# Sixteen softplus stores issued from ScalarE's queue instead of the sync engine's

## The chip, the cores and the metric

The kernel runs on one core of a Trainium2 chip. The metric is the device time of one execution in microseconds (us), as the median of several runs. Engines are named as in the profile: PE is TensorE (matmuls), PEld its weight loads, DVE is VectorE, ACT is ScalarE, POOL is GpSimd and SP is the sync engine, which here only issues DMAs. A name with a q behind it (SPq, ACTq) is the engine's sequencer, which waits for semaphores and issues DMAs.

## The reference

Three layers follow each other, on 2304 tokens of 512 features:

```python
x = attn(q, k, v, omega)            # random-feature attention, 4 x 8 heads x 576 x 64 -> (2304, 512)
h = x @ w_in                        # (2304, 512) @ (512, 2048)
g = maximum(h, 0) + log1p(exp(-abs(h)))   # softplus
x = g @ w_out                       # (2304, 2048) @ (2048, 512)
out = ((x @ w1) * (x @ w2) @ w3) @ w_out2   # 512 -> 1024 -> 1024 -> 512
```

## The kernel before, in words

Everything is kept transposed: features on the 128 partitions, tokens along the free axis. Each fp32 operand of a matmul is split into a high and a low part (`hi`, `lo`), ACT casting the high part and DVE subtracting it for the low one, and each product is three matmuls (`mm3`, line L87 in the profile).

**The softplus layer** (`widen(Up1, ...)`). The 2048 output features are 8 column pairs `i` (two blocks of 128 each), the tokens 3 chunks `c` of 768 (two halves of `N` = 384). One pair and one chunk make a quad (i,c): a two by two block product that is done with seven products and additions. `begin` does four of the seven products, copies one of them out of PSUM (`p6`, L482, on ACT), adds on DVE (`u2`, `u3`, `c22`, L475) and puts the first result; `finish` does the other three and puts three more. `put` is a softplus on ACT (L507) and a store of 128 x 384 to the DRAM tile `gd` (L508). `widen` begins a quad before it finishes the one ahead of it. The order of the last six quads is (6,0), (6,1), (7,0), (7,1), (6,2), (7,2).

**The down projection** (`down`, first use `d1`) reads `gd` back in tiles `dn` of 128 x 512 (L574, issued by SP), splits each into `dhi` (ACT, L581) and `dlo` (DVE, L582), and multiplies with `w_out`. Its `seq` takes the first two token groups together, so the `dn` tiles alternate between tokens 0 to 511 and 512 to 1023, and each tile has 12 matmuls. It loads four tiles ahead (`AHEAD`), and these four loads and the first two splits are written just before the last two quads are finished (`before_last`); the fifth load on stands in the loop behind the quads.

**Weights** are prepared on the way. A `Job` loads a raw 64-bit tile (L120, issued by ACT) and turns it into fp32 with one ACT operation (L127) and four DVE operations (L130, L136, L143, L150), then splits it (ACT L176, DVE L181). In the stretch around the change these are the jobs of `w_out`; `step(rate)` hands out such operations between products.

**What sets the order.** The framework draws up each engine's instruction list when the kernel is built, from data dependences, free buffers and priorities; `tc.high_priority(URGENT)` puts the softplus, the additions and the splits of `dn` 300 places ahead of where they are written, while stores and loads keep their own place. On the chip each engine, and each DMA queue, takes its list in order. The tiles `c22`, `c21`, `c12`, `c11`, `p6`, `u2`, `u3`, `dn`, `dhi` and `dlo` all come from one pool of 14 buffers (`M_`), and a buffer comes free when its last reader is done, for a softplus result when its store has landed.

Of the kernel before, what the change touches and what calls it, by code (L numbers as in the profile page):

```python
# [31 lines left out]
KD, NF, NJ = DM // 128, FF1 // 128, FF2 // 128  # L32
# [12 lines left out]
N = 384  # L45
# [17 lines left out]
def body(ctx: ExitStack, tc: tile.TileContext, q, k, k_rest, v, v_rest, om_t, w_in, w_out, w12, w3, wo, out):  # L63
    nc = tc.nc
# [32 lines left out]
    gd = [dr.tile([128, NT], F32, name=f"gd{f}") for f in range(NF)]  # L97
# [14 lines left out]
    class Job:  # L112
        def __init__(self, src, n, place, pool, sums=False):
            self.src, self.n, self.place, self.pool, self.sums, self.done = src, n, place, pool, sums, False
            self.slots = 4 if sums else 2
            self.kept = self.queue = None
# [382 lines left out]
    class Up1(Quad):  # L499
        def __init__(self, i, c, rate):  # L500
            super().__init__(win[i], xo[c], rate)
            self.i, self.t = i, 2 * N * c

        def put(self, dst, src, f, t):
            t = self.t + t * N
            with tc.high_priority(URGENT):
                nc.scalar.activation(out=dst, in_=src, func=AF.Softplus)  # L507
            nc.sync.dma_start(out=gd[2 * self.i + f][:, t:t + N], in_=dst)  # L508

        def begin(self):  # L510
            super().begin()
# [371 lines left out]
```

## Time and profile before

| what | value |
|---|---|
| median of 3 runs | 866.73 us (866.51 to 868.63) |
| the profiled execution's own time | 865.56 us |
| its span, from the first to the last instruction | 863.7 us |
| PE busy | 845.2 us, 98% of the span |
| DVE busy | 605.7 us, 70% |
| ACT busy | 381.8 us, 44% |
| mean granted PE clock | 0.996 of full speed |
| `gd` stores (L508), all issued by SP | 96, 192 KB each, median 2.6 us to landing |

The page gives busy time by engine over the whole span. Matmuls are pipelined, so a busy PE isn't PE at its peak, and idle time of an engine that isn't the bottleneck costs nothing. The softplus quads run from about 159 us (the first L507) to 338 us (the last L508), the first down projection from there to about 574 us.

### The profile page before, as it was taken

How to read it: one execution, taken by the hardware profiler on the slowest of the kernel's cores; microseconds unless marked ns; L12 is line 12 of the kernel's file. 1: busy time of each engine (PE TensorE's matmuls, PEld its weight loads, DVE VectorE, ACT ScalarE, POOL GpSimd, SP SyncE). 2: the span in 40 equal slices, each digit the busy share in tenths (PEclk: the TensorE clock that was granted, in tenths of full speed). 3: DMA queues.
4: the chain of work that ended last, by engine and by line, in shares of the span. 5: the costliest groups of instructions: out<-in, count | busy, mean ns of one | idle time of the engine just before them, and what ended most of it. 6: DMA issues, size and time to landing. Idle time of an engine off the chain costs nothing.

```text
span 863.7 us, 14514 instructions
## 1 busy us (share of the span) xinstructions
PE 845.2 (98%) x5496; PEld 760.6 (88%) x5496; DVE 605.7 (70%) x1007; ACT 381.8 (44%) x796; POOL 43.5 (5%) x35
## 2 busy tenths in 40 slices
PE   8999999989999998999999999999999999999998
PEld 7888888989999996888888888899999999988887
DVE  5678798978888789887876767279996655653322
ACT  6686889554444555444433432254311111232221
POOL 3512230000000000000000000000000000000000
PEclk9999999999999999999999999999999999999999
DMA  8622344564454568657687764154232211454433
GB/s 305 237 92 76 117 153 138 159 238 159 165 190 157 177 216 283 204 187 248 200 268 246 246 223 152 41 192 165 104 104 80 80 56 55 160 176 147 146 123 98
DMA packets 72534, 141.67 MB, mean 164 GB/s; under 512 B 7056, under 2 KB 39952, under 8 KB 69392
## 3 DMA queue, kind: packets, MB, share of 16 engines
q1 hardware_dynamic: 65984, 102.99, 35.7%
q10 hardware_dynamic: 6480, 37.75, 13.1%
q8 instruction: 43, 0.70, 0.3%
q14 instruction: 27, 0.22, 0.1%
HBM read 94.05 MB, written 46.66 MB: 163 GB/s over the span
## 4 chain that ended last, share of the span: by engine, by line
PE 81%; DVE 4%; DMA 3%; issue 1%; ACT 1%; SPq 0%; DVEq 0%; ACTq 0%
PE ps L87 80%; DMA xq<-xd 2%; PE ps L368 1%; PE ps L398 1%; DMA raw<-in_w_in 1%; DVE s L423 1%; DVE c L475 0%; DMA dn<-gd 0%; DMA gd<-c 0%; DVE f L143 0%; DVE u L475 0%; DVE nmax L309 0%; DVE xt L389 0%; DVE lo L181 0%; DVE dlo L582 0%
## 5 line engine op out<-in xcount | busy, mean ns | idle before, releaser
L87 PE MATMUL ps<-dlo,hi 128*128 128x512 f32 (+1 forms) x320 | 120.2, 376 | 2.9 <-DVE dlo L582 2.9
L87 PE MATMUL ps<-dhi,hi 128*128 128x512 f32 (+1 forms) x320 | 119.5, 376 | 1.6 <-ACT dhi L581 0.9
L87 PE MATMUL ps<-dhi,lo 128*128 128x512 f32 (+1 forms) x320 | 119.9, 375 | 0.0
L582 DVE TENSOR_TENSOR dlo<-dn,dhi 128x512 fp32r<-128x512 f32 (+1 forms) x120 | 74.8, 636 | 60.2 <-ACT dhi L581 33.5
L581 ACT CAST dhi<-dn 128x512 fp32r<-128x512 f32 (+1 forms) x120 | 67.4, 577 | 72.8 <-DVE dlo L582 35.4
L87 PEld LDWEIGHTS ps<-dlo,hi 128*128 128x128 f32 x320 | 60.6, 189 | 15.5 <-DVE dlo L582 3.9
L87 PEld LDWEIGHTS ps<-dhi,hi 128*128 128x128 f32 x320 | 60.3, 189 | 15.0 <-DVE c L475 1.6
L475 DVE TENSOR_TENSOR c<-ps,u 128x384 f32<-128x384 f32 x144 | 71.6, 549 | 0.6
L87 PEld LDWEIGHTS ps<-dhi,lo 128*128 128x128 f32 x320 | 60.6, 189 | 11.7
L482 ACT COPY p<-ps 128x384 f32<-128x384 f32 x48 | 22.8, 475 | 99.5 <-PE ps L87 78.0
L475 DVE TENSOR_TENSOR u<-ps,p 128x384 f32<-128x384 f32 x48 | 26.7, 555 | 56.5 <-PE ps L87 55.6
L507 ACT ACTIVATE c<-c 128x384 f32<-128x384 f32 x72 | 35.3, 522 | 67.4 <-DVE c L475 56.0
L130 DVE SCALAR_TENSOR_TENSOR f<-raw,f 128x1024 f32<-128x1024 f32 (+2 forms) x43 | 45.7, 1066 | 27.0 <-ACT f L127 26.9
L127 ACT ACTIVATE f<-raw 128x1024 f32<-128x1024 f32 (+2 forms) x43 | 42.4, 992 | 44.1 <-DMA raw<-in_w 36.2
L309 DVE TENSOR_REDUCE nmax<-ps 128x4 f32<-128x512 f32 x72 | 48.1, 682 | 18.5 <-PE ps L87 11.9
L87 PE MATMUL ps<-dhi,w34l 128*128 128x512 f32 (+1 forms) x160 | 59.6, 373 | 0.0
L87 PE MATMUL ps<-dlo,w34h 128*128 128x512 f32 (+1 forms) x160 | 59.6, 372 | 0.0
L87 PE MATMUL ps<-dhi,w34h 128*128 128x512 f32 (+1 forms) x160 | 59.1, 373 | 0.0
L176 ACT CAST hi<-f 128x1024 fp32r<-128x1024 f32 (+2 forms) x42 | 38.4, 918 | 40.1 <-DVE f L150 20.5
L181 DVE TENSOR_TENSOR lo<-f,hi 128x512 fp32r<-128x512 f32 (+3 forms) x58 | 42.0, 745 | 6.9 <-ACT hi L176 6.9
L143 DVE SCALAR_TENSOR_TENSOR f<-raw,f 128x1024 int32<-128x1024 int32 (+2 forms) x43 | 45.3, 1056 | 0.6
L150 DVE SCALAR_TENSOR_TENSOR f<-raw,f 128x1024 int32<-128x1024 int32 (+2 forms) x43 | 44.9, 1046 | 0.4
(147 smaller groups left out, 2112.2 us busy)
## 6 DMA issues: line engine op xcount, KB each, us to landing
gd<-c SPq DMA_DIRECT2D x96, 192.0 KB, 2.6
dn<-gd SPq DMA_DIRECT2D x64, 256.0 KB, 3.5
raw<-in_w ACTq DMA_DIRECT2D x16, 1024.0 KB, 6.0
pd<-c SPq DMA_DIRECT2D x48, 192.0 KB, 1.9
dn<-pd SPq DMA_DIRECT2D x32, 256.0 KB, 3.3
raw<-in_w_out ACTq DMA_DIRECT2D x10, 768.0 KB, 4.5
raw<-in_w_in ACTq DMA_DIRECT2D x6, 1024.0 KB, 5.6
rawq<-in_q SPq DMA_DIRECT2D x18, 256.0 KB, 3.7
```

Source lines behind the costliest of these rows:

```text
L87: nc.tensor.matmul(out=o, lhsT=a, rhs=b, start=start, stop=stop, **kw)
L127: nc.scalar.activation(out=self.f, in_=self.words(1, F32), func=AF.Relu, scale=-1.0)
L130: nc.vector.scalar_tensor_tensor(out=self.f, in0=self.words(1, F32), scalar=SMALLEST, in1=self.f, op0=ALU.max, op1=ALU.max)
L143: nc.vector.scalar_tensor_tensor(out=fi, in0=self.words(1, I32), scalar=-0x40000000, in1=fi, op0=ALU.bitwise_and, op1=ALU.bitwise_or,)
L150: nc.vector.scalar_tensor_tensor(out=fi, in0=self.words(0, I32), scalar=29, in1=fi, op0=ALU.logical_shift_right, op1=ALU.bitwise_or,)
L176: nc.scalar.copy(out=self.hi, in_=self.f)
L181: nc.vector.tensor_tensor(out=self.lo[:, a:b], in0=self.f[:, a:b], in1=self.hi[:, a:b].bitcast(F32), op=ALU.subtract)
L309: nc.vector.tensor_reduce(out=nmax, in_=pj, axis=AX.X, op=ALU.max, negate=True)
L475: nc.vector.tensor_tensor(out=z, in0=bank, in1=y, op=ALU.add)
L507: nc.scalar.activation(out=dst, in_=src, func=AF.Softplus)
L581: nc.scalar.copy(out=hi, in_=got[m])
L582: nc.vector.tensor_tensor(out=lo, in0=got.pop(m), in1=hi.bitcast(F32), op=ALU.subtract)
```

## The change

The stores of the quads with `i` of 6 or 7 and `c` of 1 or 2 are issued by ACT (`nc.scalar`) and not by SP (`nc.sync`). That is four quads of four stores each. Their sources, destinations and sizes stay as they are, and the other 80 stores stay on SP.

```diff
         def __init__(self, i, c, rate):
             super().__init__(win[i], xo[c], rate)
             self.i, self.t = i, 2 * N * c
+            self.queue = nc.scalar if i >= NF // 2 - 2 and c else nc.sync
 
         def put(self, dst, src, f, t):
             t = self.t + t * N
             with tc.high_priority(URGENT):
                 nc.scalar.activation(out=dst, in_=src, func=AF.Softplus)
-            nc.sync.dma_start(out=gd[2 * self.i + f][:, t:t + N], in_=dst)
+            self.queue.dma_start(out=gd[2 * self.i + f][:, t:t + N], in_=dst)
```

## Rows read from the trace of the kernel before

**Rows 1.** Windows: stretch, length, busy PE, PEld, DVE, ACT, POOL, clock, DMA share, GB/s.
```profile
178.00:316.00 138.00, 137.66 (x792) 137.48 (x793) 114.37 (x183) 68.06 (x126) 0.00 (x0) 1.00 0.53 182
...
316.00:318.00 2.00, 2.00 (x13) 2.00 (x12) 1.61 (x3) 0.16 (x1) 0.00 (x0) 1.00 0.00 0
...
329.50:342.00 12.50, 8.31 (x31) 4.81 (x29) 12.05 (x18) 8.21 (x15) 0.00 (x0) 1.00 0.78 253
342.00:346.60 4.60, 4.60 (x14) 3.60 (x14) 3.43 (x5) 2.70 (x5) 0.00 (x0) 0.63 1.04 378
346.60:574.00 227.40, 227.37 (x1029) 185.40 (x1027) 157.75 (x211) 89.38 (x135) 0.00 (x0) 1.00 0.62 204
```

**Rows 2.** Timeline of PE, 329 to 344 us: start, duration, instruction, idle before.
```profile
330.37 0.73 PE L87 MATMUL ps<-dhi,hi 128*128 128x512 f32 x2 [0.57 <-ACT dhi L581]
...
341.92 0.50 PE L87 MATMUL ps<-dlo,hi 128*128 128x512 f32 x1 [2.22 <-DVE dlo L582]
...
343.67 0.63 PE L87 MATMUL ps<-dlo,hi 128*128 128x512 f32 x1
```

**Rows 3.** Timeline of DVE in the same stretch.
```profile
329.84 0.96 DVE L130 SCALAR_TENSOR_TENSOR f<-raw,f 128x768 f32<-128x768 f32 x1 [0.50 <-ACT f L127]
...
338.45 0.95 DVE L181 TENSOR_TENSOR lo<-f,hi 128x768 fp32r<-128x768 f32 x1
```

**Rows 4.** Groups by line on DVE, 329.5 to 342 us: count, busy us, mean ns.
```profile
L130 DVE SCALAR_TENSOR_TENSOR f<-raw,f 128x768 f32<-128x768 f32 x2 | 1.9, 956 | 0.5 <-ACT f L127 0.5
...
L136 DVE TENSOR_SCALAR f<-f 128x768 int32<-128x768 int32 x2 | 1.1, 555 | 0.0
```

**Rows 5.** Timeline of ACT and its sequencer, 322 to 339 us.
```profile
322.96 0.33 ACTq L120 DMA_DIRECT2D raw<-in_w_out  x1
326.98 0.53 ACT L507 ACTIVATE c<-c 128x384 f32<-128x384 f32 x1 [3.25 <-DVE c L475]
328.91 0.91 ACT L127 ACTIVATE f<-raw 128x768 f32<-128x768 f32 x1 [1.40 <-DMA raw<-in_w_out]
...
334.80 0.91 ACT L127 ACTIVATE f<-raw 128x768 f32<-128x768 f32 x1
335.82 1.00 ACT L507 ACTIVATE c<-c 128x384 f32<-128x384 f32 x2
...
337.10 0.84 ACT L176 CAST hi<-f 128x768 fp32r<-128x768 f32 x1
337.11 0.33 ACTq L120 DMA_DIRECT2D raw<-in_w_out  x1
337.84 1.14 ACT L581 CAST dhi<-dn 128x512 fp32r<-128x512 f32 x2
```

**Rows 6.** Landing, us: raw loads of 322.96 and 317.90, first two `dn` loads.
```profile
raw<-in_w_out ACTq DMA_DIRECT2D x1, 768.0 KB, 5.9
...
raw<-in_w_out ACTq DMA_DIRECT2D x1, 768.0 KB, 4.1
...
DMA to landing us min/median/max: 3.4/3.8/4.2
```

**Rows 7.** Timeline of SP's queue, 322 to 345 us (merged runs of one line).
```profile
322.06 1.03 SPq L574 DMA_DIRECT2D dn<-gd  x2
327.54 0.32 SPq L508 DMA_DIRECT2D gd<-c  x1
327.95 0.87 SPq L574 DMA_DIRECT2D dn<-gd  x2
333.93 4.67 SPq L508 DMA_DIRECT2D gd<-c  x6
338.69 6.38 SPq L574 DMA_DIRECT2D dn<-gd  x6
```

**Rows 8.** Line L508, 296 to 340 us: ns min/median/max of one issue.
```profile
L508 SPq DMA_DIRECT2D gd<-c x23: 319/383/1275, 298.3 to 338.2; - x23
```

**Rows 9.** Line L166, all of its issues: ns min/median/max.
```profile
L166 ACTq DMA_DIRECT2D wf<-f x4: 366/432/468, 448.9 to 508.4; - x4
```

## The prediction

> **What bounds the kernel now.** I read the busy time by stage first. TensorE (PE) is the bound nearly everywhere: from 178 to 316 us, through the quads of the softplus layer, it is busy for 137.66 of 138.00 us, and from 346.6 to 574 us, in the first down projection, for 227.37 of 227.40 [rows 1]. Between them lies one knot, from 329.5 to 342 us, where the last quads end and the down projection starts: PE is busy there for 8.31 of 12.50 us, and VectorE (DVE) for 12.05. All sixteen moved stores are issued before the end of this knot, so what the change can do to the time, it does by moving the point at which PE restarts for good, 341.92 us [rows 2].
>
> Next the timeline of PE: the longest of its waits, 2.22 us, ends at 341.92 with the low part `dlo` of the third `dn` tile, and a matmul of 343.67 us takes 0.63 us where that of 341.92 took 0.50; the mean granted clock of 342 to 346.6 us is 0.63 [rows 1], so part of this stretch, right behind an idle PE, ran at the lower of the two levels (1.2 GHz). So the most that a perfect knot could give back is 12.50 - 8.31 = 4.19 us of idle time and 4.60 x (1 - 0.63) = 1.70 us of clock: 5.9 us, 0.68% of the span. Within 0.3%, or 2.6 us, is what I count as no change.
>
> Then what `dlo` waits for. The idle time of DVE in the knot, 12.50 - 12.05 = 0.45 us, is one piece, the end of the 0.50 us before 329.84, where its L130 waits for ScalarE's (ACT's) L127 [rows 3]; from there on it is gapless. Its list there is not only urgent work: two of each of L130, L136, L143 and L150 prepare `w_out` for later (L143 and L150 take 0.95 us, as L130 does) [rows 4]. Before that L127 ACT sat idle 1.40 us for the raw weight tile, whose load was issued at 322.96 us [rows 5] and took 5.9 us, where the load before it took 4.1 [rows 6].
>
> Last the queue of the sync engine (SP). It issues in order, and a store waits there for its softplus, so what is queued behind it waits too: the loads of the third and fourth `dn` tile go at 327.95, behind a store of 327.54, and the loads from the fifth on at 338.69, behind six stores that begin at 333.93 [rows 7].
>
> **The change part by part.** It moves sixteen stores, those of the quads (6,1), (7,1), (6,2) and (7,2), at a median of 0.383 us of issue each [rows 8], from SP to ACT: 6.1 us. Nothing is computed differently, and no bytes are added.
>
> *Off SP.* Left in front of the first `dn` loads are the stores of (7,0) alone. The DMA engines moved 0 GB/s from 316 to 318 us [rows 1], so the first four `dn` loads (1 MB in all) can start there, as far as their buffers are free, and not two from 322.06 and two from 327.95 [rows 7]. Their own landing was not what PE waited for: the first two landed 4.2 us after their issue at the latest [rows 6], by some 326.8, and PE started on the first at 330.37 [rows 2], when ACT had cast it; and PE needs the fifth only after the 24 matmuls of the third and fourth. So the earlier loads by themselves give 0. Indirectly they clear the way for the raw tile: two of them no longer run beside it, and I let it take the 4.1 us of its neighbour. It lands at 327.1 and not at 328.9; L127 then starts behind the softplus that ends at 327.51 [rows 5], ends at 328.4, and L130 follows the instruction before it without the 0.50 us of idle time. From there DVE is gapless to the `dlo` on which PE restarts: -0.50 us. The 0.57 us that PE waited for the first cast [rows 2] also goes, but PE only comes sooner to the same wait; it is not added. The dip of the clock I leave as it is. The bounds of this term are 0 (the loads wait for buffers, and the raw tile is as late as before) and -0.50.
>
> *Onto ACT, in the PE-bound stretch.* Nine of the sixteen fall before 322 us. If a store is put right behind its softplus, ACT's sequencer waits out the 0.53 us of it [rows 5] and issues for 0.38, where the next softplus would have started after 0.47 (two in a row take 1.00): 0.44 us, with the hand-over 0.5 each, and 2 us in a quad of 42 matmuls, 42 x 138.00 / 792 = 7.3 us. ACT is busy for 68.06 of 138.00 us there [rows 1], 3.6 in a quad, so 5.6 of 7.3 are full; PE, which never idles there, covers it. Without that cover the nine would cost 4.5 us. The raw load of 322.96 stands on the same queue and could slip by some 0.6 us; the margin that the 4.1 us leave (1.8 us) takes it.
>
> *Onto ACT, in the knot.* Seven are left: one behind the softplus of 326.98, where ACT idles 1.40 us anyway, and twice three. Cheapest: each is issued beside a running ACT operation, as the raw load at 337.11 goes beside the cast of 337.10, with the next cast at 337.84, before that one has ended (337.10 + 0.84) [rows 5]; the stores that ACT issues already, L166, take 0.37 to 0.47 us of issue [rows 9], also less than a cast. Then the cost is 0. With each three in a clump behind its last softplus it is more: with everything 0.50 us earlier, the first clump ends at about 335.1, L127 (0.91) goes from 335.1 to 336.0, the softplus from 335.82 on, three by 337.10, go from 336.0 to 337.3, the second clump ends at 338.15, and the cast L176 of 337.10, which would have gone at 336.6, ends at 339.0. DVE's L181, due at 338.45 - 0.50 = 337.95 [rows 3], starts 1.1 us late, and `dlo` with it. Dearest: seven times 0.5 us and one long issue (1.275 us at the worst [rows 8], 0.9 above the median), all in series: 4.4 us. I take 0: the rows in which ACT issues a DMA are nearest, and all show it beside a running operation. The clump's +1.1 stays in the forecast's own range.
>
> Sum: -0.50 + 0 = -0.5 us. The profiled execution took 865.56 us (span 863.7), the median of the runs is 866.73; both lie on the same kernel, and the difference is put on the median: 866.2. The forecast's own range, with both bounds of both terms, is 866.2 to 867.8 (0 and +1.1).
>
> The page "DMA: Bandwidth & Descriptors" of the Trainium skill, section "Issuing engines are not separate DMA queues", speaks against a gain: DMAs from SP and from ScalarE run on the same 16 engines, and starting them from several places saves only the sequencer's issue time. By that rule the change would save SP 6.1 us that no wait of PE shows, and the time would stay at 866.7. The row of the SP queue shows something beside it, that a load was held not by issue time but by a waiting store.
>
> **The rivals.**
>
> *The knot comes loose (faster).* Each engine's order is drawn up when the kernel is built, by priority and readiness, and the preparation of `w_out` fills holes in it. The sixteen issues now fill holes on ACT that L127 (334.80) and L176 (337.10) filled. If this L127 falls behind the casts of the third `dn` tile, the four DVE operations that hang on it (3 x 0.956 + 0.555 = 3.4 us [rows 4]) fall behind `dlo` too. They stand in front of it now, and its cast was done at about 338.5. Then the 2.22 us wait closes, the dip of the clock behind it (1.70) need not come, and with the 0.50 the time is 866.7 - 4.4 = 862.3. For it speaks that DVE alone holds `dlo`; against it that the third cast, at 337.84, needs PE to have finished with earlier tiles, which no queue changes.
>
> *ACT becomes the knot (slower).* A store that stands right behind its softplus stops every later cast on ACT, and the casts feed DVE, which has no slack in the knot. It decides from 2.6 + 0.5 = 3.1 us on, which is six of the seven stores exposed at 0.5 us and a little of a long issue; in full it is 4.4 - 0.5 = +3.9: 869.3 to 870.6. For it: the softplus that a store waits for ends later than the next one could start. Against it: ACT is busy for only 8.21 of 12.50 us in the knot [rows 1], so some of the stores fall into idle time.
>
> *Nothing moves.* The loads wait for buffers, the stores for ACT's holes, and the static order of DVE stays: 866.7.
>
> **How the numbers follow.** The forecast (866.2 and its clump variant) gets 0.38, nothing moves 0.18, the knot comes loose 0.28, ACT becomes the knot 0.16. Hence faster by over 0.3% 0.28, within 0.56, slower 0.16. The likeliest is 866.2. The range reaches from 862.0, just past the loose knot at its worked-out size (what it leaves out there is a knot that closes wholly, down to 866.7 - 5.9 = 860.8, some 0.06), to 869.5, where ACT as the knot begins; most of that case, 0.14, stays out.
>
> **What would show it.** The loads L574 of the first `dn` tiles issued before 320 us, from an SP without waits between them; the raw load of about 322.9 landing in some 4 us; no idle time of DVE at its L130; PE's last wait of the knot still about 2 us and ending 0.5 us earlier; sixteen ACT issues of L508, each about 0.38 us. Wrong would be: the order of L130 to L150 against `dlo` L582 changed, the clock's dip gone or a second one there, the waits of ACT's L176 or L581 on its own stores in place of DVE, or PE idle before 329 us, which would put the nine earlier stores on the path.

## The result, and the profile after

The change made the kernel faster: 860.37 us (857.63 to 862.58, 6 runs) against 867.68 us (864.68 to 872.78, 6 runs) for the kernel before on the same chip. The ratio is 0.9916, with a 95% interval of 0.9888 to 0.9944, so 7.3 us less, of which the interval allows 4.9 to 9.7. The forecast was 866.2, that is 0.5 us less than the 866.73 it was worked out from, with a range from 862.0 to 869.5: the time lies below the range. The profiled execution took 857.63 us, with a span of 855.6.

In `after` the lines behind 502 are numbered one higher: L507 is L508, L508 is L509, L574, L581 and L582 are L575, L582 and L583. The kernels of the experiments have some lines more, so their numbers are shifted a little further; the names of the tiles tell which line is meant.

Windows of the changed kernel (columns as in [rows 1]). The knot begins about 1 us earlier here, which comes from the attention stage and not from the change, so its window does too:

```profile
178.00:316.00 138.00, 138.00 (x796) 137.82 (x795) 112.18 (x181) 67.41 (x125) 0.00 (x0) 1.00 0.52 183
...
328.50:341.00 12.50, 11.61 (x50) 9.13 (x50) 11.50 (x18) 7.12 (x14) 0.00 (x0) 1.00 0.83 286
...
346.60:574.00 227.40, 227.40 (x1061) 187.02 (x1060) 167.05 (x224) 92.50 (x142) 0.00 (x0) 1.00 0.62 209
```

PE is busy in the knot for 11.61 of 12.50 us, where it was 8.31, and the lower clock behind it is gone. DVE is busy between 346.6 and 574 us for 9.3 us more than before (167.05 against 157.75 [rows 1]). That stretch of time doesn't hold the same work in both kernels, since the changed one is some 7 us ahead there. So here is DVE (third of the busy times) between the same two matmuls of the down projection, the 97th and the 941st, in the kernel before (first line) and in the changed one:

```profile
359.43:581.81 222.38, 222.10 (x1037) 182.63 (x1036) 152.55 (x204) 86.68 (x132) 0.00 (x0) 1.00 0.61 202
352.23:574.06 221.83, 221.83 (x1038) 182.57 (x1037) 163.29 (x219) 90.18 (x138) 0.00 (x0) 1.00 0.62 209
```

It is 10.7 us more, while PE takes no longer: work has moved from in front of the 97th matmul to behind it.

The timeline of PE from the last matmuls of the quads on:

```profile
328.51 0.33 PE L87 MATMUL ps<-xa12h,lo 128*128 128x384 f32 x1
328.68 0.63 PE L87 MATMUL ps<-dhi,hi 128*128 128x512 f32 x2
...
332.53 0.50 PE L87 MATMUL ps<-dhi,hi 128*128 128x512 f32 x1 [0.89 <-ACT c L508]
...
336.36 0.40 PE L87 MATMUL ps<-dlo,hi 128*128 128x512 f32 x1
```

PE goes from the quads into the down projection without a wait. The kernel before had five, here by what ended them (sum, number, longest):

```profile
PE ps L87 <- DVE dlo L582: 2.6, 2, 2.2
PE ps L87 <- ACT dhi L581: 0.9, 2, 0.6
PE ps L87 <- DVE c L475: 0.7, 1, 0.7
```

One is left, 0.89 us in the place of the 0.7, and the third tile's `dlo` makes none.

The timelines of DVE and of ACT show why:

```profile
327.03 1.29 DVE L583 TENSOR_TENSOR dlo<-dn,dhi 128x512 fp32r<-128x512 f32 x2 [0.24 <-ACT dhi L582]
328.24 1.02 DVE L475 TENSOR_TENSOR c<-ps,u 128x384 f32<-128x384 f32 x2
329.17 0.95 DVE L130 SCALAR_TENSOR_TENSOR f<-raw,f 128x768 f32<-128x768 f32 x1
...
334.22 0.69 DVE L583 TENSOR_TENSOR dlo<-dn,dhi 128x512 fp32r<-128x512 f32 x1 [0.97 <-ACT dhi L582]
```

```profile
326.39 0.60 ACT L582 CAST dhi<-dn 128x512 fp32r<-128x512 f32 x1
...
326.90 0.62 ACT L582 CAST dhi<-dn 128x512 fp32r<-128x512 f32 x1
327.42 0.90 ACT L127 ACTIVATE f<-raw 128x768 f32<-128x768 f32 x1
330.37 0.91 ACT L127 ACTIVATE f<-raw 128x768 f32<-128x768 f32 x1 [2.05 <-DMA raw<-in_w_out]
331.19 0.92 ACT L508 ACTIVATE c<-c 128x384 f32<-128x384 f32 x2
...
333.58 0.61 ACT L582 CAST dhi<-dn 128x512 fp32r<-128x512 f32 x1
```

The first cast, the first `dlo` and the third `dlo` (with the fourth) in the kernel before, from its timelines of ACT and of DVE:

```profile
329.71 0.61 ACT L581 CAST dhi<-dn 128x512 fp32r<-128x512 f32 x1
```

```profile
330.72 0.68 DVE L582 TENSOR_TENSOR dlo<-dn,dhi 128x512 fp32r<-128x512 f32 x1
...
341.18 1.29 DVE L582 TENSOR_TENSOR dlo<-dn,dhi 128x512 fp32r<-128x512 f32 x2
```

The first two tiles are split while PE still works on the quads. Before, an L127 that waited for its raw tile stood in front of the first cast, and an L130 in front of the first `dlo` [rows 3, 5]. Not the speed of an operation has changed but the place at which it stands. How far the preparation of the weights had come is counted by L150, the last operation of each job: those that start ahead of the first `dlo`, in the kernel before (first fence) and in the changed one:

```profile
L150 DVE SCALAR_TENSOR_TENSOR f<-raw,f x13: 948/959/1224, 186.5 to 328.4; 128x768 int32<-128x768 int32 x7, 128x1024 int32<-128x1024 int32 x6
```

```profile
L150 DVE SCALAR_TENSOR_TENSOR f<-raw,f x12: 946/1086/1225, 185.6 to 323.2; 128x1024 int32<-128x1024 int32 x6, 128x768 int32<-128x768 int32 x6
```

The count begins at 178 us. Thirteen became twelve: at the first `dlo` the preparation is one `w_out` job behind, which is five DVE operations of some 4.4 us in all (with the split L181).

The two queues, in the changed kernel's timeline of SP and its lines of L509:

```profile
297.75 14.48 SPq L509 DMA_DIRECT2D gd<-c  x7
313.94 35.77 SPq L575 DMA_DIRECT2D dn<-gd  x14
```

```profile
L509 SPq DMA_DIRECT2D gd<-c x80: 319/384/2164, 160.8 to 311.8; - x80
...
L509 ACTq DMA_DIRECT2D gd<-c x16: 326/359/871, 297.8 to 335.8; - x16
```

SP's last store is the one of 311.8 us, and its loads go from 313.94 on, before 320 us as forecast; an issue takes ACT's sequencer 0.36 us at the median.

**A measure for the knot.** Whole runs of one kernel spread by several us, so the profiles are compared by one stretch: from the start of the last matmul of the quads to the start of the 97th of the down projection. Without any wait it takes 0.17 + 96 x 0.233 = 22.5 us, from the steps between the starts of matmuls.

| kernel | from, us | to, us | stretch | PE idle in it | L150 ahead of the first `dlo` | ratio of times to the kernel before on the same chip, 95% interval |
|---|---|---|---|---|---|---|
| before | 329.46 | 359.43 | 29.97 | 4.18 | 13 | |
| before again (e12) | 330.69 | 360.63 | 29.94 | 4.34 | 13 | 1.0023 (0.9993 to 1.0053) |
| change | 328.51 | 352.23 | 23.72 | 0.89 | 12 | 0.9916 (0.9888 to 0.9944) |
| change again (e5) | 334.42 | 358.04 | 23.62 | 0.78 | 12 | 0.9930 (0.9899 to 0.9961) |
| e1 loads on GpSimd | 330.74 | 359.64 | 28.90 | 4.70 | 13 | 1.0030 (0.9995 to 1.0064) |
| e2 one job held | 333.30 | 359.70 | 26.40 | 2.29 | 13 | 0.9980 (0.9950 to 1.0011) |
| e3 two jobs held | 331.53 | 356.86 | 25.33 | 1.99 | 13 | 0.9955 (0.9923 to 0.9986) |
| e4 stores on GpSimd | 332.04 | 357.65 | 25.61 | 1.64 | 13 | 0.9992 (0.9966 to 1.0017) |
| e6 order only | 333.60 | 356.32 | 22.72 | 0 | 12 | 0.9924 (0.9899 to 0.9949) |
| e7 change, old order | 332.57 | 357.02 | 24.45 | 1.34 | 12 | 0.9934 (0.9907 to 0.9960) |
| e8 change, L127 held | 332.12 | 354.69 | 22.57 | 0 | 12 | 0.9907 (0.9871 to 0.9944) |
| e9 second chunk only | 332.54 | 358.06 | 25.52 | 1.63 | 12 | 0.9946 (0.9921 to 0.9970) |
| e10 third chunk only | 329.53 | 354.00 | 24.47 | 1.65 | 12 | 0.9945 (0.9917 to 0.9973) |
| e11 all stores on ACT | 331.62 | 354.39 | 22.77 | 0 | 10 | 0.9925 (0.9898 to 0.9953) |

The ratios are worked out over the runs and need not be those of the two medians. Of the 7.3 us, 29.97 - 23.72 = 6.25 us lie in this stretch; the rest is inside the interval. Each row rests on one profile, but both kernels that were profiled twice give the same stretch to 0.1 us.

### The profile page after: what moved, and what is told of

It is laid out like the page before. It is cut to its first block, busy times and chain, and to the rows that moved or that the text cites. A ratio compares the mean times of both kernels' runs of the same rounds, so it can differ in the third digit from the quotient of the medians.

```text
span 855.6 us, 14492 instructions
## 1 busy us (share of the span) xinstructions
PE 841.4 (98%) x5496; PEld 759.4 (89%) x5496; DVE 605.4 (71%) x1007; ACT 380.8 (45%) x796; POOL 44.0 (5%) x35
## 4 chain that ended last, share of the span: by engine, by line
PE 85%; DMA 2%; DVE 2%; issue 1%; ACT 1%; ACTq 0%; DVEq 0%
PE ps L87 83%; PE ps L368 1%; DMA xq<-xd 1%; PE ps L398 1%; DMA raw<-in_w_in 1%; DMA raw<-in_w_out 1%; DVE s L423 0%; DVE u L475 0%; DVE xa22l L433 0%; DVE nmax L309 0%; DVE t L157 0%; DVE xt L389 0%; DVE f L143 0%; ACT c L508 0%; ACT qp L314 0%
## 5 line engine op out<-in xcount | busy, mean ns | idle before, releaser
L583 DVE TENSOR_TENSOR dlo<-dn,dhi 128x512 fp32r<-128x512 f32 (+1 forms) x120 | 74.9, 635 | 65.4 <-ACT dhi L582 39.9
L582 ACT CAST dhi<-dn 128x512 fp32r<-128x512 f32 (+1 forms) x120 | 67.2, 576 | 59.9 <-DVE dlo L583 32.6
L87 PEld LDWEIGHTS ps<-dhi,lo 128*128 128x128 f32 x320 | 60.2, 188 | 11.7
L482 ACT COPY p<-ps 128x384 f32<-128x384 f32 x48 | 22.8, 475 | 99.1 <-PE ps L87 77.9
L508 ACT ACTIVATE c<-c 128x384 f32<-128x384 f32 x72 | 35.2, 521 | 65.9 <-DVE c L475 54.6
L130 DVE SCALAR_TENSOR_TENSOR f<-raw,f 128x1024 f32<-128x1024 f32 (+2 forms) x43 | 45.7, 1066 | 17.2 <-ACT f L127 17.0
L127 ACT ACTIVATE f<-raw 128x1024 f32<-128x1024 f32 (+2 forms) x43 | 42.3, 991 | 29.9 <-DMA raw<-in_w 21.3
L181 DVE TENSOR_TENSOR lo<-f,hi 128x512 fp32r<-128x512 f32 (+3 forms) x58 | 42.0, 745 | 8.0 <-ACT hi L176 8.0
L150 DVE SCALAR_TENSOR_TENSOR f<-raw,f 128x1024 int32<-128x1024 int32 (+2 forms) x43 | 45.0, 1046 | 0.5
```

Of the source, the lines that this page charges most:

```text
L87: nc.tensor.matmul(out=o, lhsT=a, rhs=b, start=start, stop=stop, **kw)
L127: nc.scalar.activation(out=self.f, in_=self.words(1, F32), func=AF.Relu, scale=-1.0)
L130: nc.vector.scalar_tensor_tensor(out=self.f, in0=self.words(1, F32), scalar=SMALLEST, in1=self.f, op0=ALU.max, op1=ALU.max)
L150: nc.vector.scalar_tensor_tensor(out=fi, in0=self.words(0, I32), scalar=29, in1=fi, op0=ALU.logical_shift_right, op1=ALU.bitwise_or,)
L181: nc.vector.tensor_tensor(out=self.lo[:, a:b], in0=self.f[:, a:b], in1=self.hi[:, a:b].bitcast(F32), op=ALU.subtract)
L582: nc.scalar.copy(out=hi, in_=got[m])
```

## The experiments

The theories are named in the expectations. **A**: the gain lies in the order in which the instruction lists of DVE, ACT and PE are drawn up, and the moved stores act by changing that order. **B**: it lies on the chip, in loads and buffers that no longer stand behind waiting stores in SP's queue. **B2** is B as a helper: the order helps only where the loads come earlier too.

### e1: the first four loads alone out of SP's queue

```diff
-                nc.sync.dma_start(out=got[m], in_=src[f][:, t0:t0 + n])
+                (nc.gpsimd if before and m < AHEAD else nc.sync).dma_start(out=got[m], in_=src[f][:, t0:t0 + n])
```

> All stores stay on SP; only the first four dn loads are issued from GpSimd's queue, where nothing stands in front of them. The built lists of PE, DVE and ACT are those of the kernel before, instruction for instruction. Theory A (the gain lies in the order that the lists of DVE, ACT and PE were drawn up in): the raw tile may land earlier, the last wait of PE in the knot stays about 2.2 us and the lower clock behind it too; at most 0.5 us faster than before, ratio 0.999 to 1.001. Theory B (the gain lies on the chip, in loads that no longer stand behind waiting stores in SP's queue): most of the 7 us come, ratio 0.991 to 0.994, and the 2.2 us wait is gone.

No gain: 867.8 us, ratio 1.0030. The loads did go early, in GpSimd's timeline:

```profile
318.53 1.75 POOL L574 DMA_DIRECT2D dn<-gd  x3 [184.91 <-DVE u L475]
320.88 0.54 POOL L574 DMA_DIRECT2D dn<-gd  x1 [0.61 <-DVE c L475]
```

and PE's waits did not shrink. The first grew from 0.57 to 1.06 us, the last stayed the same to the hundredth of a microsecond:

```profile
332.13 0.73 PE L87 MATMUL ps<-dhi,hi 128*128 128x512 f32 x2 [1.06 <-ACT dhi L581]
...
343.68 0.50 PE L87 MATMUL ps<-dlo,hi 128*128 128x512 f32 x1 [2.22 <-DVE dlo L582]
```

The raw tile that was to land faster took longer; its L127 in ACT's timeline, and its landing:

```profile
330.68 0.90 ACT L127 ACTIVATE f<-raw 128x768 f32<-128x768 f32 x1 [1.89 <-DMA raw<-in_w_out]
```

```profile
raw<-in_w_out ACTq DMA_DIRECT2D x1, 768.0 KB, 6.3
```

It took 6.3 us, against 5.9 in the kernel before [rows 6], with the `dn` loads issued 3.5 us and more ahead of it. The stretch is 1.07 us shorter although PE idles longer in it, since the clock did not fall this time. With the lists unchanged, the first four loads come early and the times show no gain: the interval (0.9995 to 1.0064) leaves out B's 0.991 to 0.994. The loads from the fifth on and the buffers were not freed here; e6 answers for them.

### e2 and e3: only an order, with all stores on SP

An order is added to the list of DVE: the first DVE operation of one later job (e2, the ninth), or of two (e3, the eighth and ninth), must follow the `dlo` of the fourth tile.

```diff
         def floor(self):
-            nc.vector.scalar_tensor_tensor(
+            with tc.issue_after(lows[HELD]) if self in held else ExitStack():
+                nc.vector.scalar_tensor_tensor(
...
+    lows, HELD = {}, 3
+    held += [wout[j] for j in [8]]
```

> All stores and loads stay on SP as before; one thing is added, an order on DVE: the four preparing operations of the ninth w_out job (L130 to L150) may not go before the dlo of the fourth dn tile. Theory A: dlo of the third tile comes 2.7 us earlier, right behind its cast (ends at 338.45), PE's 2.2 us wait closes and the 1.7 us of lower clock go; 3 to 4 us faster than before, ratio 0.995 to 0.9965. Theory B: SP's queue is as before, so nothing comes, ratio 0.999 to 1.001.

> As the run that holds one job, but the operations of the eighth job are held back too, which stand in front of the dlo of the first tile in the kernel before. Theory A: PE's waits at the start of the knot (0.57 and 0.35 us) shrink as well, and the whole of the change's gain comes without moving a store: 5 to 6.5 us, ratio 0.9925 to 0.9945. Theory B: ratio 0.999 to 1.001.

No load or store was moved in either. In e2 the wait of 2.2 us is gone; PE's one wait left for a `dlo` is that of the first tile, which was as long before:

```profile
PE ps L87 <- DVE dlo L584: 0.4, 1, 0.4
```

The stretch fell by 3.57 us in e2 and by 4.64 in e3. A's forecasts were of the times, and these fell by less than A had said: to 865.03 us in e2 (ratio 0.9980 against A's 0.995 to 0.9965) and to 863.39 us in e3 (0.9955 against 0.9925 to 0.9945), where the kernel before took 866.25. e2's interval reaches from A's range to 1.0011, so it settles nothing by itself; e3's, 0.9923 to 0.9986, leaves out B's 0.999 to 1.001. What e3 lacked is in its idle time of 1.99 us: PE's first wait, which A had shrinking, grew to 1.1 us, for a cast that still stood behind ACT's waiting L127 (the second, 0.35 us, is gone).

### e4: the same stores on GpSimd

```diff
-            self.queue = nc.scalar if i >= NF // 2 - 2 and c else nc.sync
+            self.queue = nc.gpsimd if i >= NF // 2 - 2 and c else nc.sync
```

> The same sixteen stores leave SP, but for GpSimd's queue, so ACT issues none. SP is as free as in the changed kernel. In the built list of DVE the low part L181 and L143 and L150 of the ninth job now stand behind the dlo of the third tile, the L130 and L136 still in front. Theory A: dlo comes up to 2.4 us earlier, the long wait closes nearly, the lower clock goes, but the waits before it stay: 3 to 4.5 us faster, ratio 0.995 to 0.9965. Theory B: as fast as the changed kernel, ratio 0.990 to 0.993. If ACT's issues were what put the preparation behind dlo, the ratio is 1.0.

SP is as free as in the change, and the time stays: 866.35 us, ratio 0.9992, which misses A's 3 to 4.5 us and B's range, and is what the last sentence of the expectation had for the case that ACT's issues push the preparation. It is not pushed back here; thirteen L150 stand ahead of the first `dlo`:

```profile
L150 DVE SCALAR_TENSOR_TENSOR f<-raw,f x13: 946/959/1226, 186.2 to 331.5; 128x768 int32<-128x768 int32 x7, 128x1024 int32<-128x1024 int32 x6
```

The stretch is 4.36 us shorter, with three operations moved behind the third `dlo`, as A had it. But DVE lost time just ahead of it, to an L127:

```profile
327.22 0.96 DVE L130 SCALAR_TENSOR_TENSOR f<-raw,f 128x768 f32<-128x768 f32 x1 [2.57 <-ACT f L127]
```

and PE waited 1.59 us for the addition behind it. By the profile 4.36 - 1.59 = 2.8 us of gain should be left; the interval of the times runs from 2.9 us of gain to 1.5 us of loss, so it just reaches that at its edge. Where the rest went stays open. The swap isn't quite clean either: a store from GpSimd took 4.4 us to landing at the median, where one from SP took 2.6. What e4 shows is that a free SP doesn't push the preparation back by a job; with the same stores on ACT, it goes back.

### e5 to e8: order and queue apart

e5 is the change once more. e6 has every store and load on SP and adds orders alone, e7 has the change's queues and puts DVE's old order back in one place, e8 adds one order to the change.

> The change itself, once more, on the chip of the next three runs, as their yardstick. Both theories: ratio 0.989 to 0.994; from the last matmul of the quads to the 97th of the down projection 23.5 to 24.5 us, where the kernel before took 30.0 and the changed one 23.7; no wait of PE above 1.2 us there.

The stretch was 23.62 us, the time 860.43 against 868.11 us, ratio 0.9930, as expected.

```diff
+            with tc.issue_after(highs[hold_high[self]]) if self in hold_high else ExitStack():
+                nc.scalar.activation(out=self.f, in_=self.words(1, F32), func=AF.Relu, scale=-1.0)
...
+    hold_low.update({wout[j]: m for j, m in {6: 1, 7: 3, 8: 4}.items()})
+    hold_high.update({wout[j]: m for j, m in {6: 1, 7: 2, 8: 3}.items()})
```

> All stores and loads on SP as in the kernel before; only orders are added, on DVE and ACT: the preparation of the seventh, eighth and ninth w_out job may not go before the splits of the second, third and fourth (dhi) or second, fourth and fifth (dlo) dn tile, so that both lists run one job behind, as they do in the changed kernel. Theory A (the gain lies in the order of the lists): the stretch of 97 matmuls falls from 30.0 to between 23.5 and 25 us, the raw wait of ACT no longer stands before the first cast, and the ratio is 0.990 to 0.994. Theory B2 (the order helps only because the loads and buffers also come earlier with SP free): 26 us or more, ratio above 0.996.

This is the run that decides. 860.58 us, ratio 0.9924 beside 0.9930 for the change on the same chip, and PE without any wait in the knot. Its windows and its SP timeline:

```profile
333.60:346.10 12.50, 12.50 (x55) 9.92 (x55) 10.33 (x15) 6.75 (x13) 0.00 (x0) 1.00 0.85 303
...
346.60:574.00 227.40, 227.34 (x1042) 185.82 (x1041) 166.95 (x225) 93.76 (x144) 0.00 (x0) 1.00 0.62 208
```

```profile
330.81 0.32 SPq L511 DMA_DIRECT2D gd<-c  x1
331.22 1.11 SPq L577 DMA_DIRECT2D dn<-gd  x2
333.03 4.52 SPq L511 DMA_DIRECT2D gd<-c  x6
337.64 10.79 SPq L577 DMA_DIRECT2D dn<-gd  x8
```

and the third cast in its timeline of ACT:

```profile
336.53 0.62 ACT L584 CAST dhi<-dn 128x512 fp32r<-128x512 f32 x1 [0.93 <-PE ps L87]
```

SP's queue is in the shape of [rows 7], two loads behind one store and the rest behind six, and PE is at its pace all the same. DVE's later share rises to 166.95 us (160.3 between the 97th and the 941st matmul, so most of the way to the change's 163.3). The stretch, 22.72 us, came out below A's 23.5 to 25; the ratio lies in A's range and below B2's. So the order helps without early loads: B2 falls, and B with it.

```diff
+            if self in first:
+                tc.add_manual_dep(
+                    lows[first[self]], last.ins.name,
+                    mybir.DependencyInfo(mybir.DependencyClass.NoSync, mybir.DependencyReason.DATA), reason="order",
+                )
...
+    first.update({wout[7]: 2})
```

> The sixteen stores stay on ACT and SP stays free, but DVE must finish the preparation of the eighth w_out job before the dlo of the third dn tile, which puts 11 operations between the dlo of the second and of the third tile and not 8 (the kernel before has 10). Theory A: the last wait of PE comes back, with 2 to 4 us, the stretch of 97 matmuls takes 26.5 to 30 us, ratio 0.996 to 1.002. Theory B2: DVE catches up since everything else is earlier, at most 1 us is lost, ratio 0.990 to 0.995.

Here A's numbers missed, and B2's came: against the change's own run the stretch lost 0.8 us, where A had it at 26.5 us or more, and the time is that of the change. The edit did put the old order back: by the traces twelve operations stand between the second and the third `dlo`, as many as in the kernel before, where the change has eight (the counts in the expectation are off). The waits of PE, and the third `dlo` in DVE's timeline:

```profile
PE ps L87 <- ACT c L514: 0.8, 1, 0.8
PE ps L87 <- DVE dlo L589: 0.6, 1, 0.6
```

```profile
340.31 0.69 DVE L589 TENSOR_TENSOR dlo<-dn,dhi 128x512 fp32r<-128x512 f32 x1
```

The `dlo` wait did come back, but small. The first two tiles are split before PE has left the quads, so the third `dlo` starts 340.31 - 332.57 = 7.7 us into the stretch; in the kernel before, with the same twelve operations, it was 341.18 - 329.46 = 11.7. So the count of operations in front of that one `dlo`, which I had taken for the cause, isn't enough: it costs little where the preparation is a job behind when the knot begins. B2 has the same number for another reason, loads from a free SP, and e7 doesn't tell the two apart; e6 does, and leaves A in this wider form.

```diff
+    hold_high.update({wout[j]: m for j, m in {7: 2}.items()})
```

> The change, and ACT's first operation of the eighth w_out job, which waits there for its raw tile for 2.05 us with three softplus of the quads behind it, is put behind the cast of the third dn tile. Theory A: the last wait of PE in the changed kernel, 0.89 us for a PSUM bank that one of these softplus frees, goes; the stretch takes 22.8 to 23.5 us and the ratio is 0.1% below that of the change. If that wait is the price of the stores on ACT, it stays.

The wait of 0.89 us is gone; PE is busy without a break:

```profile
332.10:344.60 12.50, 12.50 (x56) 10.15 (x55) 9.77 (x16) 7.55 (x15) 0.00 (x0) 1.00 0.87 292
```

The stretch, 22.57 us, is at its floor, a little below A's 22.8 to 23.5. So that wait was no price of the stores but of an L127 that waits for its raw tile with three softplus behind it. The median is 859.68 us beside 860.43; a difference of that size the intervals don't show, so e8 is better than the change in its profile and not shown to be in its time.

### e9 to e12: the parts, the whole, and the kernel before again

`c == 1` (e9) or `c == 2` (e10) takes the place of `c`, and in e11 the queue is ACT's for all quads.

> Half of the change: only the eight stores of the second chunk, (6,1) and (7,1), on ACT. They are all issued before the knot; in the knot SP's queue is as before, seven stores with the third and fourth dn load behind the first of them. The built lists run one w_out job behind those of the kernel before. Theory A: the stretch of 97 matmuls takes 23 to 26 us, ratio 0.990 to 0.995. If the stores that stand in front of the loads in the knot were the cause, 28 us or more and a ratio above 0.996.

> The other half: only the eight stores of the third chunk, (6,2) and (7,2), on ACT, seven of them in the knot. The list of DVE runs half a job to one job behind that of the kernel before. Theory A: 23 to 26 us for the stretch, ratio 0.990 to 0.995, since half of the issues is enough to push the preparation back. If it takes all sixteen, 27 us or more.

Each half pushes the preparation back by one job and gives most of the gain, 861.91 and 861.47 us against 866.53, both in A's range. In e9 the seven stores in the knot are on SP, where they were, so the gain doesn't need the loads behind them to be freed.

> All 96 stores on ACT; the lists around the knot are nearly those of the changed kernel. The prediction's step: in the stretch where PE never idles the issues are covered, so the quads take as long as before (138 us from 178 to 316) and the time is that of the changed kernel, ratio 0.989 to 0.995. Without that cover 80 issues of 0.5 us more cost up to 40 us.

859.42 us, ratio 0.9925, and a stretch at its floor. Its quads and its line L509:

```profile
178.00:316.00 138.00, 137.89 (x779) 137.13 (x778) 104.22 (x171) 65.14 (x119) 0.00 (x0) 1.00 0.47 166
```

```profile
L509 ACTq DMA_DIRECT2D gd<-c x96: 326/420/1836, 160.2 to 337.1; - x96
```

With 80 more issues PE idles 0.11 us in 138. It does start fewer matmuls there, 779 where the kernel before had 792 [rows 1], but that comes from a slower pace that shows without any issue on ACT too. The same window of the kernel before in e12:

```profile
178.00:316.00 138.00, 138.00 (x783) 137.81 (x782) 113.05 (x182) 66.79 (x124) 0.00 (x0) 1.00 0.52 180
```

The last 780 matmuls of the quads take 138.4 us in e11 and 137.9 in e12, so in these two profiles the 80 issues come with 0.5 us, and the 40 us that they would cost without cover are out. The preparation stands three jobs behind, ten L150 ahead of the first `dlo`.

> The kernel before against itself, on the chip of the other three: ratio 0.997 to 1.003. Both theories: its stretch takes 28 to 31 us, with a wait of 2.2 us at its end; whether the lower clock follows is open, 28.2 us without and 30 with it.

The same kernel gave a ratio of 1.0023, the same stretch and the lower clock behind it once more; PE's first and last wait:

```profile
331.74 0.74 PE L87 MATMUL ps<-dhi,hi 128*128 128x512 f32 x2 [0.71 <-ACT dhi L581]
...
343.29 0.79 PE L87 MATMUL ps<-dlo,hi 128*128 128x512 f32 x1 [2.21 <-DVE dlo L582]
```

## Why the prediction was wrong

**What bounds the kernel: right.** PE is the bound, only the knot can give, DVE's list holds it there, and 6.25 of the 7.3 us came from it.

**The most that the knot could give, 5.9 us: too small.** The stretch went from 29.97 to 22.57 us in the best run, 7.4 us. I had added the idle times and the clock. A matmul shows as busy for 0.40 us but the next starts after 0.23, so the 0.17 us by which each of five waits hides behind the busy time are not in the 4.19 (0.85 us in all), nor is the slower first matmul (0.50 us) behind each wait.

**Off SP, -0.50 us: wrong.** The loads went early, from 313.94 us, as described. But e1, where the first four do so with nothing else changed, has the raw tile in 6.3 us and not in 4.1, DVE's wait at L130 at 0.99 us and not at 0, and PE's last wait the same. The raw load of the row that I took as a model ran at another place of the kernel; that other loads made the difference was argued and not read.

**Onto ACT in the PE-bound stretch, covered: right.** e11 has nearly all of its 96 issues there, and PE idles 0.11 us in 138.

**Onto ACT in the knot, taken as 0: the step that failed.** The sum priced what an issue costs on the chip, and took the lists of the engines as they were. On the chip that price was indeed about 0: the one wait left had another cause (e8). But the lists did not stay. Sixteen issues on ACT put the preparation of `w_out` one job back, out of the knot and into the down projection, where DVE is busy for 167 of 227 us and nobody waits for it. That ACT's issues do it and not the freed SP is what e4 and e9 show; that an order alone is enough, e6. Two things stay open: how the framework's priorities come from ACT's issues to these lists, which no run followed, and a run with the change's exact lists and all stores on SP, since e6's order is near them and not the same.

**The rival that came true: the mechanism right, the size and chance off.** "The knot comes loose" named the issues that fill ACT's holes, the preparation falling behind `dlo`, the closed 2.22 us wait and the clock. It counted four operations in front of one `dlo`, -4.4 us; the whole list slid by a job, so the waits at the start of the knot closed too: -6.25 us. Moving those four alone is e2: the long wait closes and the stretch falls by 3.57 us. Putting the old order back in front of that `dlo`, with the list a job behind, is e7: 0.8 us. I gave the rival 0.28, for the argument that the third cast must wait for PE. In the kernel before (337.84) and in the change (333.58) that cast goes right behind ACT's operation before it and waits for nothing; in e6, where it does wait for PE, it waits 0.93 us and PE loses nothing by it. The rivals "ACT becomes the knot" and "nothing moves" did not occur.

**The rule of the Trainium skill** (page "DMA: Bandwidth & Descriptors", section "Issuing engines are not separate DMA queues") that issuing from several engines saves only the sequencer's issue time agrees with the runs as far as the chip goes: e1 and e4, where loads or stores change their queue and the preparation isn't pushed back by a job, gained nothing that the times show. The gain of the change isn't one of DMA.

## What to carry to other kernels

Where a framework draws up the lists by priority and readiness, moving an instruction to another engine can change the order on every engine; compare the lists of both kernels before pricing anything, above all low-priority work that is filled in ahead of an urgent chain. A stage change where PE waits for a busy DVE was relieved here by moving early work behind it, and an explicit order (e6) did that directly, without a DMA that changed its queue. The idle time of a pipelined engine understates what its waits cost; measure a fixed count of instructions from start to start.

## What the hardware showed that I had not expected

A wait of 2.2 us at the same place was followed by 3.4 us at the lower clock in both profiles of the kernel before, but by none in e1, whose wait is the same to the hundredth; so a price for the clock that hangs on one wait holds for some executions only. And the quads ahead of the knot don't repeat as it does: the change's two profiles have 23.72 and 23.62 us in the stretch, but 334.42 - 328.51 = 5.9 us between their starts of it. In the slower of them PE ran at the lower clock for 6.8 us near 177 us. Besides, PE has two paces in the quads, at a granted clock of 1.00 in both: the mean step from start to start of a matmul is 0.1733 us in six of the fourteen profiles and 0.1767 us in the other eight, so the last 780 matmuls take 135.3 or 137.9 us where PE waits for nothing. The same kernel shows both (before and e12, the change and e5), so it isn't the stores; what sets it stays open. With such spread, 12 runs left an interval of some 0.6% on a ratio, and the stretch told apart what the times couldn't.
